# Router products by halves of a tile, value products behind the next tile's scores, six copies moved to VectorE

## The chip, the core and the metric
The kernel runs on one core of a Trainium2 chip. A core has a matrix engine (PE, with its weight loads PEld beside it), VectorE (DVE), ScalarE (ACT), GpSimd (POOL) and a queue engine for transfers (SP). Each engine takes its own instructions in the order in which the program issues them. The metric is the device time in microseconds; all times below are microseconds unless marked otherwise.

## The reference
Three parts follow one another over 2304 tokens (4 sequences of 576) of 512 values:

```python
# 1. attention: 8 heads of 64, each query sees itself and the 63 keys before it
scores = scale * np.matmul(q, k.transpose(0, 1, 3, 2))
scores = np.where((rel >= 0) & (rel < 64), scores, -1e9)
attn = np.exp(scores - np.max(scores, -1, keepdims=True))
attn = attn / (np.sum(attn, -1, keepdims=True) + 1e-09)
x = np.matmul(attn, v)                       # then [2304, 512]
# 2. mixture of 8 experts, two for each token
noisy = x @ w_gate + np.log1p(np.exp(x @ w_noise)) * noise
top2 = ...                                   # the two largest, weights by softmax
out[token] += weight * (np.maximum(x @ w1[e], 0) @ w2[e])
# 3. a feed-forward layer of width 2048 with a piecewise quadratic gate
h = x @ w_in;  g = where(h >= 1, h, where(h <= -1, 0, (h + 1) ** 2 / 4));  return g @ w_out
```

The change touches part 1 and the first line of part 2 only: the router's products `x @ w_gate` and `x @ w_noise` (16 columns together).

## The kernel before
The first 104 us hold the attention with the router and the routing; the experts and the last layer follow and aren't touched.

Attention works on 18 tiles of 128 tokens in 36 steps (`step(u)`, two steps a tile; step u handles heads in the half `u % 2`, and `m = u // 2`). A written order rules: the engines get exactly the order of the calls in `step` (`manual_schedule`). The pieces are:

- `A(i)`, L347 to L366: the scores of a whole tile, for two steps. Four mask products (L355) and 16 products of queries and keys (L364) in 64x64 blocks. A tile's scores fill two of three score banks `Sb`, taken in turn by `u % 3` (L345). Line L364 appears with 32 instructions a tile in the trace, since each f32 product is recorded as two.
- `top(u)`, L371 and L373: the row maxima on VectorE, straight from the score bank; the scaled negative `nb` on GpSimd (from step 4).
- `soft(u)`, L380: four exponentials on ScalarE from the score bank into `p`.
- `C(u)`, L387 and L389: four transposes of `p` on PE into a bank of a pair used in turn (`rot`), and the copy `pt` on ScalarE.
- `Dm(u)`, L401 to L416, for odd u: 16 products of `pt` and the values into `OB` (weights of 128x64, so two column halves), then on VectorE the sums, the reciprocal and the scaled output `x` (L406 to L409), a store of `x`, and a copy of values on GpSimd (L415).
- `Ex(i)`, L422 and L424: four transposes of `x` into a `rot` bank and the copy `xt`, on ScalarE.
- `Gm(i)`, L440 and L443: the router's four products with weights of 128x128 from `xt` and 16 moving columns, into a `rot` bank, and a small copy on VectorE. `logits` calls it, and after the last tile of a group (8, 4 and 6 tiles) starts `route`.
- `route(g)` gives the routing of a group in portions that `advance` takes in each step, mostly on VectorE; it has position products on PE (L558 to L562, in a `rot` bank too) and puts marks (L586, L593) in a queue, which `place` (L634) turns into products.
- `split_w` and `rest_w` (L158, L149) prepare expert weights on ScalarE and VectorE at the ends of some steps (of every four steps, two have a half on ScalarE).

The order in an even step is: `A` of the next tile, `Ex` of the tile two back, `C`, the two `top`, `soft`, `place`, `early`, `advance`, `Dm` of the tile one back with its VectorE part. In an odd step: `C`, `soft`, `logits`, `place`, `early`, `advance`. On ScalarE an even step so has `xt`, `pt`, then the exponentials of `u + 2`. `early` starts the gather for the first expert's rows when the first two groups are placed. After step 36 the last router products stand between transposes for the first expert (L774 to L783).

Of the kernel before, what the change touches and what calls it, by code (L numbers as in the profile page):

```python
# [17 lines left out]
AF = mybir.ActivationFunctionType  # L18
# [8 lines left out]
E, F = 8, 1024  # L27
# [30 lines left out]
def fused_kernel(ctx, tc, qT, kT, v, wg, noise, wcat, out, wd=None):  # L58
    nc = tc.nc
# [41 lines left out]
    def load_qk(j):  # L101
        q_t[j] = qbuf[:, j % 2]
        kt = k_t[j] = qk.tile([P, 4, 320], F32, tag="k", name=f"k{j}")

        for h in (slice(0, P), slice(P, 256)) if j == 0 else (slice(0, 256),):
            t = slice(256 * j + h.start, 256 * j + h.stop)
            nc.sync.dma_start(out=kt[:, :, 64 + h.start:64 + h.stop], in_=kTv[:, :, t])
            nc.sync.dma_start(out=q_t[j][:, :, h], in_=qTv[:, :, t])
        if j == 0:
            nc.vector.memset(kt[:, :, 0:64], 0.0)  # L110


    def keys_before(j):
        nc.gpsimd.tensor_copy(k_t[j][:, :, 0:64], k_t[j - 1][:, :, 256:320])
# [4 lines left out]
    def load_v(i):  # L119
        a = vp.tile([P, H * VW], F32, tag="vE", name=f"vE{i}")  # L120
        nc.sync.dma_start(out=a, in_=v[P * i:P * i + P, :])
        if i == 0:
            vO[0] = vp.tile([P, H * VW], F32, tag="vE", name="vE_")
            nc.vector.memset(vO[0][64:128, :], 0.0)
            nc.sync.dma_start(out=vO[0][0:64, :], in_=v[0:64, :])
        vE[i] = a
# [6 lines left out]
    def load_raw(n, eng=nc.sync):  # L133
        raws[n] = t = raw.tile([P, 1024], F32, tag="raw", name=f"raw{n}")
        if NF <= n < N2:

            if n % NF == 0:
                r = E - 2 if n >= NCE else (n // NF - 1) % (E - 2)
                dyn[n // NF] = nc.values_load(cnt_i[0:1, 1 + r:2 + r], engines=[mybir.EngineType.SP], min_val=0,
                                          max_val=(E - 1) * NF)  # L140
            eng.dma_start(out=t, in_=wcat[bass.ds(dyn[n // NF] + n % NF, 1)].rearrange("o p n -> (o p) n"))
        else:
            eng.dma_start(out=t, in_=wcat[n])
# [114 lines left out]
    wg_sb = ac.tile([P, 4, 32], F32, name="wg_sb")  # L258
# [76 lines left out]
    def rot(u):  # L335
        turn[0] += 1
        return bank[3 + 2 * (turn[0] % 2)] if u <= NU else bank[6]
# [6 lines left out]
    def score(u):  # L344
        return OB[:, 0, :] if u == 3 else Sb[u % 3]  # L345
# [22 lines left out]
    def top(u):  # L368
        mx = wk.tile([P, 4], F32, tag="mx", name=f"mx{u}", bufs=3)
        nb = wk.tile([P, 4], F32, tag="nb", name=f"nb{u}", bufs=3)  # L370
        nc.vector.tensor_reduce(out=mx, in_=score(u).rearrange("p (g n) -> p g n", g=4), axis=AX.X, op=ALU.max)  # L371

        (nc.vector if u < 4 else nc.gpsimd).tensor_scalar(out=nb, in0=mx, scalar1=-0.125, scalar2=None, op0=ALU.mult)  # L373
        mxs[u] = nb

    def soft(u):
        sb, nb = score(u), mxs.pop(u)
        p = wk.tile([P, 4, P], F32, tag="p", name=f"p{u}", bufs=4)
        for g in range(4):
            nc.scalar.activation(p[:, g, :], sb[:, g * P:g * P + P], AF.Exp, bias=nb[:, g:g + 1], scale=0.125)  # L380
        pr[u] = p

    def C(u):
        p = pr.pop(u)
        PTb = rot(u)
        for g in range(4):
            nc.tensor.transpose(PTb[:, g * P:g * P + P], p[:, g, :], idn)  # L387
        t = wk.tile([P, 512], F32, tag="pt", name=f"pt{u}", bufs=PTB)
        nc.scalar.activation(t, PTb, AF.Copy)  # L389
        pts[u] = t  # L390

    def Dm(u):
        i, r = divmod(u, 2)
        if r == 0:
            return
        ts = [pts.pop(2 * i + k) for k in range(2)]
        for h in range(H):
            g, k = divmod(h, 2)
            for c in range(2):
                vv = (vO, vE)[c][i]  # L400
                nc.tensor.matmul(OB[64 * c:64 * c + 64, h // 4, (h % 4) * VW:(h % 4) * VW + VW],  # L401
                                 lhsT=ts[k][:, g * P + 64 * c:g * P + 64 * c + 64], rhs=vv[:, h * VW:h * VW + VW],
                                 start=True, stop=True)
        ov = OB[:, :, 0:4 * VW].rearrange("p b (h d) -> p b h d", d=VW)
        rl = wk.tile([P, 2, 4, 1], F32, tag="rl", name=f"rl{i}")
        nc.vector.tensor_scalar(out=rl, in0=ov[:, :, :, D:VW], scalar1=1e-9, scalar2=None, op0=ALU.add)  # L406
        nc.vector.reciprocal(out=rl, in_=rl)
        x = wk.tile([P, H, D], F32, tag="x", name=f"x{i}", bufs=3)
        nc.vector.tensor_tensor(out=x.rearrange("p (b h) d -> p b h d", b=2), in0=ov[:, :, :, 0:D],  # L409
                                in1=rl.to_broadcast([P, 2, 4, D]), op=ALU.mult)  # L410
        xs[i] = x
        nc.sync.dma_start(out=x_dram[P * i:P * i + P, :], in_=x.rearrange("p h d -> p (h d)"))
        if i + 1 < NT:
            if i + 2 < NT:
                nc.gpsimd.tensor_copy(vE[i][0:64, :], vE[i + 1][0:64, :])  # L415
            vO[i + 1] = vE[i]  # L416

    def Ex(i, u):
        x = xs.pop(i).rearrange("p h d -> p (h d)")
        XTb = rot(u)  # L420
        for k in range(4):
            nc.tensor.transpose(XTb[:, k * P:k * P + P], x[:, k * P:k * P + P], idn)  # L422
        xt = wk.tile([P, 4, P], F32, tag="xt", name=f"xt{i}")
        nc.scalar.activation(xt.rearrange("p k t -> p (k t)"), XTb, AF.Copy)  # L424
        xts[i] = xt

    gstart = [sum(GROUPS[:g]) for g in range(len(GROUPS))]
    n_early = 2 * gstart[EARLY]
# [6 lines left out]
    def Gm(i, u):  # L435
        g, t = tile_group[i]
        xt = xts.pop(i)
        lg = (rot(u) if u <= NU else bank[0])[:, LGO:LGO + 2 * E]
        for k in range(4):
            nc.tensor.matmul(lg, lhsT=xt[:, k, :], rhs=wg_sb[:, k, 0:2 * E], start=(k == 0), stop=(k == 3))  # L440
        if t == 0:
            lgs_g[g] = gp.tile([P, max(GROUPS), 2 * E], F32, tag="lgs", name=f"lgs{g}", bufs=3)
        nc.vector.tensor_copy(lgs_g[g][:, t, :], lg)  # L443
# [179 lines left out]
        state["late"] = True  # L623
        yield 1

    live, rows = [], {}

    def place():
        while pq:
            c, o, ej = pq.popleft()  # L630
            if nids[0] == n_early:
                open_ids()
            nids[0] += 1
            nc.tensor.matmul(IDS2[:, c, :], lhsT=o, rhs=ej, start=False, stop=(nids[0] in (n_early, 2 * NT)))  # L634
# [23 lines left out]
    def open_ids():  # L658
        nc.tensor.matmul(IDS[:, 0:2 * NK], lhsT=wz[:, 0:P], rhs=wz[:, 0:2 * NK], start=True, stop=False)
# [16 lines left out]
    def step(u):  # L676
        for c in range(EW):
            if u == L0 + LS * c:
                load_raw(c)
        if u + 2 < NU:  # L680
            if (u + 2) % 4 == 0 and (u + 2) // 4 + 1 < NT // 2:
                load_qk((u + 2) // 4 + 1)
                keys_before((u + 2) // 4 + 1)
            if (u + 1) % 2 == 0 and (u + 1) // 2 + 1 < NT:
                load_v((u + 1) // 2 + 1)


        m = u // 2
        if u % 2 == 0:
            if u + 2 < NU:  # L690
                A(m + 1)
            if u == NU:
                nc.scalar.activation(vE[NT - 2][0:64, :], vE[NT - 1][0:64, :], AF.Copy)
            if u == NU - 2:
                C(u)
            if 0 <= m - 2 < NT:
                Ex(m - 2, u)
        if u < NU and u != NU - 2:
            C(u)
        if u % 2 == 0 and u + 2 < NU:  # L700
            top(u + 2)
            top(u + 3)
        if u + 2 < NU:
            soft(u + 2)

        if u % 2 == 1 and 0 <= m - 2 < NT:
            logits(m - 2, u)
        place()
        early()
        advance(MARKS[u > NU - 10])  # L710
        if 0 <= u - 1 < NU:
            Dm(u - 1)

        for c in range(EW):
            for h in range(2):
                if u == L0 + LS * c + 3 + h:
                    split_w(c, h)
                if u == L0 + LS * c + 4 + h and c < EW - 2:
                    rest_w(c, slice(512 * h, 512 * h + 512))
            if u == L0 + LS * c + 4 and EW <= c + 2 < NF:  # L720
                load_raw(c + 2)
# [54 lines left out]
    warm(2, Sb[0])  # L776
    xpose("0a", 0, P, Sb[0])
    Ex(NT - 1, NU)
    xpose("0a", 1, P, Sb[1])
    logits(NT - 1, NU)  # L780
# [232 lines left out]
    t0 = 0  # L1013
# [402 lines left out]
    for q, (ui, p) in enumerate(items):  # L1416
# [5 lines left out]
        while ndone < len(items) and ndone <= q + (1 if items[ndone][0] == FIRST2 else 2):  # L1422
            i = items[ndone]
# [84 lines left out]
```

## Time and profile before

| | |
|---|---|
| median of 3 runs | 947.45 (947.38 to 947.93) |
| the profiled execution | 950.02, its span 948.3 |
| PE busy | 935.7, 99% of the span |
| VectorE busy | 665.6, 70% |
| ScalarE busy | 436.5, 46% |
| GpSimd busy | 186.2, 20% |
| TensorE clock granted | 1.0 of full speed in all slices |

Busy times are those of one profiled execution; times in a timeline count from the start of its span. A matmul's end is modelled, so a busy PE can have work overlapping; the weight loads tell better when one group follows another. A bracket at the end of a row is the idle time just before it and what ended it.

### The profile page before, as it was taken

To read this page: it belongs to the slowest core of one execution; us is meant where nothing else is said; L and a number is where in the kernel's file an instruction comes from. 1 tells how busy PE (TensorE), PEld (TensorE's weight loads), DVE (VectorE), ACT (ScalarE), POOL (GpSimd) and SP (SyncE) were. 2 spreads that over 40 slices of the span, in tenths; PEclk is the share of its full clock that TensorE was granted. 3 is DMA by queue.
4 is the path that set the end of the run, shared out by engine and by line. 5 is a ranking of instruction groups with operands and counts; after the bars stand their busy time and mean duration, and the time that the engine had idled before them with its cause. 6 is when DMAs were issued, how large, how long until landed. Compare 5 with 4: busy or idle time off the path is not lost. (4 is left out here: it accounts for less than half of the span.)

```text
span 948.3 us, 17990 instructions
## 1 busy us (share of the span) xinstructions
PE 935.7 (99%) x6779; PEld 832.3 (88%) x6781; DVE 665.6 (70%) x1411; ACT 436.5 (46%) x907; POOL 186.2 (20%) x249
## 2 busy tenths in 40 slices
PE   9999999999999999999999999999999999999998
PEld 6887888988888989898888889988999899899986
DVE  4689765477997968889533366767867776687664
ACT  6898314345565555555433266333433333342221
POOL 3222013133645353354402030000000000000000
PEclk9999999999999999999999999999999999999999
DMA  8874136555888878767725566775576559556521
GB/s 258 300 252 167 56 100 186 188 191 199 290 288 275 261 236 277 257 206 260 252 89 184 204 231 236 252 256 178 177 256 213 164 174 308 175 178 213 182 95 44
DMA packets 91274, 196.95 MB, mean 208 GB/s; under 512 B 7320, under 2 KB 18072, under 8 KB 91184
## 3 DMA queue, kind: packets, MB, share of 16 engines
q1 hardware_dynamic: 83152, 171.68, 54.6%
q0 software_dynamic: 6736, 21.86, 6.4%
q10 hardware_dynamic: 1296, 2.23, 0.6%
q8 instruction: 54, 0.88, 0.4%
q14 instruction: 36, 0.29, 0.1%
HBM read 155.45 MB, written 40.29 MB: 206 GB/s over the span
## 5 line engine op out<-in xcount | busy, mean ns | idle before, releaser
L969 PE MATMUL bank<-wo,hall 128*128 128x512 f32 x864 | 237.6, 394 | 0.0
L969 PE MATMUL bank<-w,hall 128*128 128x512 f32 (+3 forms) x944 | 234.6, 396 | 0.1
L969 PEld LDWEIGHTS bank<-w,hall 128*128 128x128 f32 (+3 forms) x944 | 167.7, 183 | 35.2 <-issue 0.3
L969 PEld LDWEIGHTS bank<-wo,hall 128*128 128x128 f32 x864 | 146.7, 188 | 17.4 <-DVE hall L915 0.2
L904 ACT ACTIVATE hall<-bank 128x288 fp32r<-128x288 f32 (+6 forms) x128 | 54.0, 422 | 218.4 <-PE bank L896 200.6
L896 PE MATMUL bank<-xhie,w 128*128 128x288 f32 (+4 forms) x768 | 122.5, 302 | 0.3 <-DVE hall L907 0.2
L896 PEld LDWEIGHTS bank<-xhie,w 128*128 128x128 f32 x768 | 113.5, 188 | 7.1 <-DVE hall L907 1.4
L907 DVE SCALAR_TENSOR_TENSOR hall<-bank,hall 128x288 fp32r<-128x288 f32 (+7 forms) x168 | 60.0, 391 | 82.5 <-ACT hall L904 75.1
L149 DVE TENSOR_TENSOR w<-raw,w 128x1024 fp32r<-128x1024 f32 (+1 forms) x69 | 81.9, 1188 | 23.8 <-ACT w L158 17.8
L1183 PEld LDWEIGHTS bank<-xb,wi 128*128 128x128 f32 x576 | 80.8, 188 | 8.4 <-DVE cg L1173 0.7
L1207 ACT ACTIVATE hall<-cg 128x512 fp32r<-128x512 f32 x64 | 40.3, 629 | 100.4 <-DVE cg L1205 100.4
L1183 PE MATMUL bank<-xb,wi 128*128 128x256 f32 x576 | 84.3, 282 | 0.3 <-DVE cg L1173 0.3
L1183 PEld LDWEIGHTS bank<-xc,wi 128*128 128x128 f32 x480 | 67.5, 188 | 6.5
L1183 PE MATMUL bank<-xc,wi 128*128 128x256 f32 x480 | 69.9, 280 | 0.0
L158 ACT ACTIVATE w<-raw 128x1024 fp32r<-128x1024 f32 (+1 forms) x71 | 69.4, 977 | 0.0
L896 PE MATMUL bank<-xloe,w 128*128 128x288 f32 (+4 forms) x384 | 69.0, 301 | 0.0
L1201 ACT ACTIVATE mg<-cg 128x512 f32<-128x512 f32 x64 | 40.1, 626 | 45.8 <-DVE cg L1173 44.1
L204 POOL TENSOR_TENSOR td<-rawd 128x512 f32<-128x512 f32 x32 | 33.3, 1040 | 139.6 <-DVE rawd L202 111.8
L896 PEld LDWEIGHTS bank<-xloe,w 128*128 128x128 f32 x384 | 58.0, 188 | 0.0
L1202 DVE SCALAR_TENSOR_TENSOR cg<-mg,cg 128x512 f32<-128x512 f32 x64 | 43.8, 684 | 18.8 <-ACT mg L1201 18.8
L1211 DVE SCALAR_TENSOR_TENSOR hall<-cg,hall 128x512 fp32r<-128x512 f32 x64 | 44.0, 687 | 8.1 <-ACT hall L1207 7.7
L1205 DVE SCALAR_TENSOR_TENSOR cg<-mg,cg 128x512 f32<-128x512 f32 x64 | 44.0, 687 | 1.0
(285 smaller groups left out, 1389.2 us busy)
## 6 DMA issues: line engine op xcount, KB each, us to landing
wi<-w1o SPq DMA_DIRECT2D x56, 1024.0 KB
raw<-wcat SPq DMA_DIRECT2D x64, 512.0 KB
rawd<-wd SPq DMA_DIRECT2D x32, 512.0 KB
w1o<-so SPq DMA_DIRECT2D x64, 256.0 KB
y<-y_dram SPq DMA_DIRECT2D x28, 256.0 KB
vE<-v SPq DMA_DIRECT2D x18, 260.0 KB
x_dram<-x SPq DMA_DIRECT2D x18, 256.0 KB
k<-kT SPq DMA_DIRECT2D x8, 512.0 KB
```

The costliest lines, as they stand in the source:

```text
L149: nc.vector.tensor_tensor(out=w[:, 1, c], in0=t[:, c], in1=w[:, 0, c].bitcast(F32), op=ALU.subtract)
L158: nc.scalar.activation(w[:, 0, c], t[:, c], AF.Copy)
L896: nc.tensor.matmul(ps, lhsT=l[k], rhs=r[:, k, s:s + w], start=(c == 0), stop=(c == len(prods) - 1))
L904: nc.scalar.activation(hh, ps, AF.Relu)
L907: nc.vector.scalar_tensor_tensor(out=t, in0=ps[:, c], scalar=0.0, in1=hh[:, c].bitcast(F32), op0=ALU.max, op1=ALU.subtract)
L969: nc.tensor.matmul(M2[b][0:w], lhsT=h2[:, o:o + w], rhs=r[n], start=(first and a == 0), stop=(last and a == end))
L1183: nc.tensor.matmul(ps, lhsT=w[:, l, k * P:k * P + P], rhs=r[:, m, k, :], start=(c == 0), stop=(c == len(prods) - 1))
L1201: nc.scalar.activation(st["m"], c, AF.Relu, scale=0.5)
L1202: nc.vector.scalar_tensor_tensor(out=c, in0=st["m"], scalar=1.0, in1=c, op0=ALU.min, op1=ALU.subtract)
L1205: nc.vector.scalar_tensor_tensor(out=c, in0=st["m"], scalar=1.0, in1=c, op0=ALU.min, op1=ALU.mult)
L1207: nc.scalar.activation(h2[:, 0:T], c, AF.Copy, scale=-1.0)
L1211: nc.vector.scalar_tensor_tensor(out=h2[:, T:2 * T], in0=c, scalar=-1.0, in1=h2[:, 0:T].bitcast(F32), op0=ALU.mult, op1=ALU.subtract)
```

## The change
The router's products are issued for tokens 0 to 63 and 64 to 127 apart, so eight products with weights of 128x64 in place of four with 128x128. `Dm` loses its VectorE part, the store and the copy of values to a new `norm`, which stays at the end of the step; from step 4 on the products of `Dm` are issued right behind `A` and ahead of `Ex` and `C`. For tiles 0 to 5 the copy `xt` goes to VectorE and is issued behind the two `top` of its step. In odd steps `place` comes before `logits`.

```diff
@@ Dm / norm
                                  start=True, stop=True)
+
+    def norm(u):
+        i, r = divmod(u, 2)
+        if r == 0:
+            return
         ov = OB[:, :, 0:4 * VW].rearrange("p b (h d) -> p b h d", d=VW)
@@ Ex
-        nc.scalar.activation(xt.rearrange("p k t -> p (k t)"), XTb, AF.Copy)
         xts[i] = xt
+        if i < 6:
+            behind_tops.append(lambda: nc.vector.tensor_copy(xt.rearrange("p k t -> p (k t)"), XTb))
+        else:
+            nc.scalar.activation(xt.rearrange("p k t -> p (k t)"), XTb, AF.Copy)
@@ Gm
         for k in range(4):
-            nc.tensor.matmul(lg, lhsT=xt[:, k, :], rhs=wg_sb[:, k, 0:2 * E], start=(k == 0), stop=(k == 3))
+            for t0 in (0, 64):
+                s = slice(t0, t0 + 64)
+                nc.tensor.matmul(lg[s], lhsT=xt[:, k, s], rhs=wg_sb[:, k, 0:2 * E], start=(k == 0), stop=(k == 3))
@@ step
                 nc.scalar.activation(vE[NT - 2][0:64, :], vE[NT - 1][0:64, :], AF.Copy)
+            if u > 2:
+                Dm(u - 1)
             if u == NU - 2:
                 C(u)
@@
             top(u + 2)
             top(u + 3)
+        while behind_tops:
+            behind_tops.popleft()()
         if u + 2 < NU:
             soft(u + 2)
 
+        place()
         if u % 2 == 1 and 0 <= m - 2 < NT:
             logits(m - 2, u)
-        place()
         early()
         advance(MARKS[u > NU - 10])
         if 0 <= u - 1 < NU:
-            Dm(u - 1)
+            if u <= 2:
+                Dm(u - 1)
+            norm(u - 1)
```

## Rows read from the trace of the kernel before
**Rows 1.** The page's first part: busy time, share of the span, instructions.
```profile
PE 935.7 (99%) x6779; PEld 832.3 (88%) x6781; DVE 665.6 (70%) x1411; ACT 436.5 (46%) x907; POOL 186.2 (20%) x249
```
**Rows 2.** Waits of PE from 100 us on: total, times, longest.
```profile
PE bank L761 <- DVE xloe L768: 2.2, 1, 2.2
```
**Rows 3.** Timeline of the weight loads, one tile: start, duration, operation, idle before.
```profile
43.77 0.11 PEld L355 LDWEIGHTS <-id 64*64 64x64 bf16 x4
...
44.99 0.42 PEld L422 LDWEIGHTS bank<-idn,x 128*128 128x128 f32 x4 [0.17 <-ACT p L380]
45.38 0.47 PEld L387 LDWEIGHTS bank<-idn,p 128*128 128x128 f32 x4
46.01 1.01 PEld L401 LDWEIGHTS ob<-vE,pt 128*64 128x64 f32 x32 [0.17 <-issue]
47.09 0.42 PEld L387 LDWEIGHTS bank<-idn,p 128*128 128x128 f32 x4
47.48 0.97 PEld L440 LDWEIGHTS bank<-wg_sb,xt 128*128 128x128 f32 x8
48.48 0.11 PEld L355 LDWEIGHTS <-id 64*64 64x64 bf16 x4
```
**Rows 4.** The same timeline: the first loads of A3 and of A13.
```profile
15.34 0.24 PEld L355 LDWEIGHTS <-id 64*64 64x64 bf16 x4 [0.17 <-issue]
...
62.60 0.11 PEld L355 LDWEIGHTS <-id 64*64 64x64 bf16 x4
```
**Rows 5.** Timeline of all engines in step 2: A waits for a score bank.
```profile
10.62 1.21 ACT L380 ACTIVATE p<-bank,nb 128x128 f32<-128x128 f32 x4
...
11.88 0.40 PE L355 MATMUL bank<-mask,id 64*64 64x512 bf16 x2 [0.85 <-ACT p L380]
...
13.08 0.42 PEld L387 LDWEIGHTS bank<-idn,p 128*128 128x128 f32 x4 [0.17 <-issue]
```
**Rows 6.** Timeline of ACT in the tile of rows 3.
```profile
45.69 0.60 ACT L424 ACTIVATE xt<-bank 128x512 f32<-128x512 f32 x1 [0.91 <-PE bank L422]
46.18 0.59 ACT L389 ACTIVATE pt<-bank 128x512 f32<-128x512 f32 x1
46.66 1.15 ACT L380 ACTIVATE p<-bank,nb 128x128 f32<-128x128 f32 x4
47.65 0.67 ACT L158 ACTIVATE w<-raw 128x512 fp32r<-128x512 f32 x1
48.17 0.63 ACT L389 ACTIVATE pt<-bank 128x512 f32<-128x512 f32 x1
```
**Rows 7.** Timeline of PE in the same tile.
```profile
44.99 0.66 PE L422 MATMUL bank<-idn,x 128*128 128x128 f32 x4
45.48 0.60 PE L387 MATMUL bank<-idn,p 128*128 128x128 f32 x4
```
**Rows 8.** Timeline of DVE in the same tile.
```profile
45.19 1.29 DVE L371 TENSOR_REDUCE mx<-bank 128x4 f32<-128x512 f32 x2 [0.85 <-PE bank L364]
```
**Rows 9.** Groups by line, DVE, 0 to 250 us: busy us, mean ns, idle before.
```profile
L988 DVE COPY ye<-bank 128x512 f32<-128x512 f32 x3 | 2.1, 688 | 1.0 <-PE bank L969 1.0
```
**Rows 10.** Timeline of PE, the position products of the first group.
```profile
67.67 0.19 PE L558 MATMUL bank<-ohs,tri 128*128 128x64 bf16 x1 [0.30 <-ACT pt L389]
```
**Rows 11.** Timeline of DVE in the routing part and the tail.
```profile
69.89 1.28 DVE L371 TENSOR_REDUCE mx<-bank 128x4 f32<-128x512 f32 x2
...
88.13 1.28 DVE L371 TENSOR_REDUCE mx<-bank 128x4 f32<-128x512 f32 x2
...
95.90 0.69 DVE L409 TENSOR_TENSOR x<-ob,rl 128x512 f32<-128x512 f32 x1
```
**Rows 12.** Busy time by stretch: length, PE, PEld, DVE, ACT, POOL, clock, DMA, GB/s.
```profile
70.00:80.00 10.00, 9.73 (x183) 8.36 (x181) 9.76 (x39) 9.97 (x32) 2.20 (x6) 1.00 0.79 286
```
**Rows 13.** Timeline of PE in the tail.
```profile
96.73 0.63 PE L422 MATMUL bank<-idn,x 128*128 128x128 f32 x4 [0.65 <-ACT pt L389]
...
101.46 1.06 PE L440 MATMUL bank<-wg_sb,xt 128*128 128x16 f32 x8 [0.45 <-ACT xt L424]
```

More of the change, by code (lines that the diff above doesn't have):

```diff
@@ L624, in bump @@
         yield 1
-    live, rows = [], {}
+    live, rows, behind_tops = [], {}, deque()
     def place():
```

## The prediction
> **What bounds the kernel now.** I read the page first, then the timeline of the attention stage engine by engine, then the waits in it. The page gives PE 99% busy over the span [rows 1], so the reader should ask of any edit whether PE, which takes its instructions in order, gets to the first feed-forward product earlier or later. After about 104 us PE is filled by the feed-forward and its longest wait there, 2.2 us [rows 2], is for rows gathered by what the routing found, so it too follows from the attention stage: a shift of that stage should move the end by the same amount.
>
> The attention stage runs in pairs of steps, one tile a pair. One pair in the weight loads [rows 3]: masks and scores A at 43.77, turned output Ex 44.99, turned probabilities C 45.38, values Dm 46.01, second C 47.09, router Gm 47.48, next A 48.48. Each group starts as the one before it ends, so this stage is PE's own work: 4.71 a tile. From A3 at 15.34 to A13 at 62.60 [rows 4] it is 47.26 for ten tiles, 4.73 each.
>
> Behind that lies a second loop, which decides here. There are three score banks, and A writes two of them; its third mask product needs the bank whose four exponentials were queued on ACT one pair earlier. That the kernel waits there by name is seen in step 2: exponentials 10.62 + 1.21 = 11.83, mask product at 11.88 with 0.85 idle, released by ACT p [rows 5]. ACT takes its queue in order too: in an even step it does xt (from Ex), then pt (from C), then those exponentials [rows 6]. So the loop is A, Ex, C, pt, exponentials, A. Measured from the release of A's third mask: 1.20 to the next group's load (13.08 less 11.88, [rows 5]); Ex's four products end 0.66 after its load, 45.65 [rows 7]; xt starts 0.04 later (45.69), pt 0.49 after that, the exponentials 0.48 after that, they last 1.15 [rows 6], and A follows 0.05 after: 1.20 + 0.66 + 0.04 + 0.49 + 0.48 + 1.15 + 0.05 = 4.07. The rows agree: exponentials end at 47.81, A starts 48.48, so 0.67 is to spare.
>
> **The change part by part.**
>
> *Values' products moved.* From step 4 on, Dm stands between A and Ex. PE's total isn't changed by it, but the loop is: Dm now lies ahead of C, C ahead of pt, pt ahead of the exponentials for which the next A waits. Queued behind Dm on PE are Ex and both C; who waits for those is ACT, with pt and the exponentials behind. Dm's price is 1.08 (46.01 to 47.09, [rows 3]). New loop, without an xt on ACT: A to Dm 1.20, Dm 1.08, Ex to C 0.39 (44.99 to 45.38), C's load to its last product 0.70 (45.38 to 46.08, [rows 3, 7]), then 0.04, 0.48, 1.15, 0.05 = 5.09. With xt on ACT: 1.20 + 1.08 + 0.66 + 0.04 + 0.49 + 0.48 + 1.15 + 0.05 = 5.15. Both are above 4.73, so the 0.67 is used up and PE stands idle before A.
> The term that no row shows is the turn from A (64x64 blocks) to Dm (128x64). After A the load engine shows 0.17 idle, before Ex as before C [rows 3, 5]; from Gm to A it is only 0.03 (48.45 to 48.48). I take 0.17, the row with the same predecessor; with 0.03 the loops are 4.95 and 5.01.
> Dm's own input is no later wait: the exponentials occupy ACT for 0.99, a weight split for 0.52 (46.66 to 47.65 to 48.17, the pt row [rows 6]), pt 0.63, so the second pt ends about 6.1 after the old release, and Dm needs it at 5.09 + 1.20 = 6.29.
>
> *Router by halves.* 8 loads of 128 columns in 0.97 become 16 of 64 columns. Dm loads 32 of that very shape in 1.01, 0.032 each [rows 3], so 16 take 0.51: 0.46 less. Against it, going from C into 64-column blocks costs 0.63 (45.38 to 46.01) where C to Gm cost 0.39. So PE saves 0.2 net, in a stretch in which, by the loop above, it waits anyway. Worth nothing in the loop; by itself it lies between a gain of 0.22 a tile and a loss of 0.24 (the turn paid and no load shortened).
> The Trainium skill, TensorE: Matmul & The Clock Gate, Part 3 (packing small matmuls), says that a weight load overlaps running products only where the row groups differ. The two halves share all rows, and by that the 16 loads would take as long as the 8 did, a rival below. The trace speaks against it: Dm's 32 loads share all rows too and went at 0.032 each.
>
> *Turned output copied by VectorE, six tiles.* It removes xt from ACT, and in the new order that is worth only the 0.06 between 5.15 and 5.09, since pt waits for C. On DVE it comes behind both maxima (they end 2.71 after A's load: 45.19 + 1.29 less 43.77, [rows 8]), starts when Ex ends (1.20 + 1.08 + 0.66 = 2.94, and 0.13 for the hand-over, my allowance of three times ScalarE's 0.04), and takes 0.69, the nearest copy from PSUM of that shape [rows 9]: done 3.76. The second C takes that bank, so: 3.81, C to Gm 0.63, Gm 0.51, 0.03 = 4.98, under 5.09 by 0.11. That is its cover. The maxima stay ahead of it, and nb on POOL with them.
> Placing ahead of the router costs nothing until step 26, when there are first marks.
>
> *Sum of the light part.* Steps 4 to 14 are six periods of 5.09, steps 16 to 22 four of 5.15: 51.14 against 47.26, +3.9. With the smaller turn 6 x 4.95 + 4 x 5.01 = 49.74, +2.5.
>
> *Routing part, 62.6 to 88.* At the end of step 25 the position product takes the bank of the second C and already waited for its pt (0.30 at 67.67, [rows 10]), 5.07 after A13. In the new order the exponentials start at 3.95 (1.20 + 1.08 + 0.66 + 0.04 + 0.49 + 0.48), so that pt comes at 3.95 + 0.99 + 0.52 = 5.46, ends 6.09, and the product starts 6.14: 1.07 later. VectorE reads it next, so +1.0. From there the maxima come at 69.89 and 88.13 [rows 11], 18.24 for three tiles, 6.08 each, with DVE 9.76 busy of 10 [rows 12]: above 5.15, so VectorE sets this stretch as before and the delay is only handed on. Bounds 0.3 and 1.0.
>
> *Tail.* The last tiles have no A, so Dm ahead is a gain: x for tile 16 came at 96.59 (95.90 + 0.69, [rows 11]) and Ex began at 96.73 after a wait; its row names ACT pt, but x was what came last [rows 13]. With Dm in front, x is ready before, but Dm of the last tile now waits for its pt and ACT's copy of the values first, so most of it is lost: I count 0.3. The router products after 98 stand on PE's path (101.46, [rows 13]) and give 0.4. Together -0.7, bounds 0 and -1.5.
>
> Sum: +3.9 + 1.0 - 0.7 = +4.2. The profiled execution took 950.02 (span 948.3), 2.6 above the median 947.45; the difference is carried to the median: 951.6.
>
> **Rivals.**
> *Faster: the score wait does not bind.* If A did not have to wait for the exponentials behind pt, PE's own sum would rule: 1.22 + 1.08 + 0.39 + 0.39 + 0.63 + 0.54 = 4.25, 0.48 a tile less; ten tiles -4.8, the tail -0.7, time 942. For it: PE at 99% and 0.2 to 0.46 truly removed. Against it: step 2 shows this very wait, and the order on ACT is not altered. It decides from the point at which the exponentials end less than 4.7 after the release. Chance 0.12.
> *No change.* The turn costs 0.03 (+2.5), the delay of the position product is eaten by VectorE's shorter backlog (0), the tail gives its full 1.5: +1.0, 948.5. For it: DVE gets idle time in the light part. Against it: all three must fall one way. Chance 0.10.
> *Slower still: the halves don't overlap.* Then Gm lasts 0.97, and PE's path behind the turned output is 3.81 + 0.63 + 0.97 + 0.03 = 5.44 in six tiles and, with xt on ACT (2.98 + 0.60 + 0.05 = 3.63 in place of 3.81), 5.26 in four: 6 x 0.35 + 4 x 0.11 = 2.5 more, 954.1. Against it stands Dm's pace. Chance 0.08.
>
> **How the numbers follow.** My forecast has 0.70. Its own range is +1.3 (2.5 + 0.3 - 1.5) to +4.9, 948.7 to 952.4. The range takes in no change and the halves without overlap and leaves out the faster case: 947.5 to 954.5. About 0.2% (1.9 us) is what can be told from no change. Slower is the forecast without its low end and the third rival, 0.77; same is the second rival and a little, 0.11; faster 0.12.
>
> **What would show it.** In the light part A to A should read about 5.1, with PE idle 0.3 or more before or inside the masks, released by ACT p; Ex and C should start some 2.3 and 2.7 after A; the router's 16 loads should take about 0.5. DVE should hold six copies of about 0.69 right behind the maxima, with pt no earlier for it. The position product of step 25 should wait longer for pt. I am wrong if A to A is under 4.7 there, or if PE shows no wait for ACT p, or if the stage's loss does not reach the first feed-forward product.

## The result, and the profile after

The changed kernel takes 954.62 (median of 6 executions, 953.81 to 955.12); the kernel before, timed beside it, 947.94 (947.38 to 948.96). The ratio is 1.0072 with a 95% interval of 1.0061 to 1.0083: slower by 6.7 where 4.2 was forecast, and 0.1 above the forecast's range of 947.5 to 954.5. The profiled execution took 953.81.

First the page: busy time, share of the span, instructions [rows 1]. PE is busy for 1.8 less and the span is 3.8 longer, so the change has bought waits.

```profile
span 952.1 us, 18293 instructions
...
PE 933.9 (98%) x6923; PEld 828.3 (87%) x6925; DVE 670.2 (70%) x1417; ACT 433.3 (46%) x901; POOL 185.1 (19%) x249
```

The waits of PE between 15 and 110 us name them (engine, line, bank waited for and releaser: total, times, longest).

```profile
PE bank L387 <- DVE rl L411: 3.0, 6, 0.5
PE bank L568 <- ACT pt L389: 2.1, 2, 1.3
PE bank L387 <- ACT xt L433: 1.3, 5, 0.3
PE bank L644 <- DVE ohe L603: 1.2, 1, 1.2
PE bank L644 <- ACT ohe L606: 1.2, 1, 1.2
PE bank L450 <- ACT xt L433: 1.1, 2, 0.7
```

New line numbers: `Ex` L427, `xt` L431 on VectorE and L433 on ScalarE, sums and scaling L411 to L414, router L450, position products L568, marks L596 to L606, `place` L644. The stage, cut where A's first mask loads, against [rows 4] and the other A's of the same timeline:

| stretch | before | after | difference | forecast |
|---|---|---|---|---|
| start to A3 | 15.34 | 15.06 | -0.28 | 0 |
| A3 to A13, ten light tiles | 47.26 | 51.06 | +3.80 | +3.9 |
| A13 to A14, position products of group 0 | 5.38 | 6.82 | +1.44 | |
| A14 to A17 | 17.02 | 17.65 | +0.63 | |
| A13 to A17, routing part | 22.40 | 24.47 | +2.07 | +1.0 |
| A17 to the first feed-forward load | 18.73 | 19.26 | +0.53 | -0.7 |
| sum, at that load | 103.73 | 109.85 | +6.12 | +4.2 |

The spans differ by only 3.8 because the wait of 2.2 in [rows 2] is absent from the profile after: from that load to the end it takes 842.25 where the profile of before takes 844.58. That profile of before, at 950.02, was 2.1 above the median; so the 6.12 is what to set against the 6.7 between medians, and 0.6 of it is left unassigned.

One tile in the light part, weight loads (start, duration, operation, idle before), as [rows 3]. The first line is the second C of the last tile with `xt` on VectorE; from 48.13 on, `xt` is on ScalarE:

```profile
44.60 0.42 PEld L387 LDWEIGHTS bank<-idn,p 128*128 128x128 f32 x4 [0.71 <-issue]
45.19 0.55 PEld L450 LDWEIGHTS bank<-wg_sb,xt 128*64 128x64 f32 x16 [0.17 <-issue]
45.77 0.18 PEld L355 LDWEIGHTS <-id 64*64 64x64 bf16 x4
...
47.05 1.01 PEld L401 LDWEIGHTS ob<-vE,pt 128*64 128x64 f32 x32 [0.17 <-issue]
48.13 0.42 PEld L427 LDWEIGHTS bank<-idn,x 128*128 128x128 f32 x4
48.52 0.47 PEld L387 LDWEIGHTS bank<-idn,p 128*128 128x128 f32 x4
49.47 0.42 PEld L387 LDWEIGHTS bank<-idn,p 128*128 128x128 f32 x4 [0.49 <-ACT xt L433]
50.06 0.55 PEld L450 LDWEIGHTS bank<-wg_sb,xt 128*64 128x64 f32 x16 [0.17 <-ACT pt L389]
50.63 0.11 PEld L355 LDWEIGHTS <-id 64*64 64x64 bf16 x3
50.99 0.10 PEld L355 LDWEIGHTS <-id 64*64 64x64 bf16 x1 [0.25 <-issue]
...
55.79 0.11 PEld L355 LDWEIGHTS <-id 64*64 64x64 bf16 x3
```

The period is 51.06 / 10 = 5.11 (5.10 each from 25.37 to 45.77; 5.16 from 50.63 to 55.79). The 16 loads of the router take 0.55. In the tile at 50.63 the mask is cut in two: three loads, then 0.25 idle, and the fourth as ScalarE's exponentials end (ACT, as [rows 6]; 49.80 + 1.15 = 50.95):

```profile
48.83 0.60 ACT L433 ACTIVATE xt<-bank 128x512 f32<-128x512 f32 x1 [1.52 <-PE bank L427]
49.32 0.59 ACT L389 ACTIVATE pt<-bank 128x512 f32<-128x512 f32 x1
49.80 1.15 ACT L380 ACTIVATE p<-bank,nb 128x128 f32<-128x128 f32 x4
```

In the tiles with the copy on VectorE the second C waits 0.51 for it (DVE and PE). The row of PE names the next DVE instruction (44.41 to 44.56), but that one reads `OB`; the bank that C takes is the one the copy reads until 44.49:

```profile
43.80 0.69 DVE L431 COPY xt<-bank 128x512 f32<-128x512 f32 x1 [0.40 <-PE bank L427]
```
```profile
44.63 0.63 PE L387 MATMUL bank<-idn,p 128*128 128x128 f32 x4 [0.51 <-DVE rl L411]
```

The score bank still holds A in these tiles, though little: the exponentials end at 45.79 (ACT), and the four mask loads at 45.77 take 0.18 where they take 0.11 in [rows 3].

```profile
44.66 1.13 ACT L380 ACTIVATE p<-bank,nb 128x128 f32<-128x128 f32 x4
```

The routing part and the tail (PE, as [rows 10, 13]): four waits, and behind the last one products that last longer than the same ones elsewhere.

```profile
72.63 0.19 PE L568 MATMUL bank<-ohs,tri 128*128 128x64 bf16 x1 [1.29 <-ACT pt L389]
...
83.59 0.65 PE L644 MATMUL bank<-ohe,ohr 128*128 128x145 f16 x4 [1.17 <-ACT ohe L606]
...
90.39 0.18 PE L568 MATMUL bank<-ohs,tri 128*128 128x32 bf16 x1 [0.77 <-ACT pt L389]
...
96.06 0.65 PE L644 MATMUL bank<-ohe,ohr 128*128 128x145 f16 x4 [1.17 <-DVE ohe L603]
96.64 0.65 PE L450 MATMUL bank<-wg_sb,xt 128*64 128x16 f32 x16
97.23 1.56 PE L401 MATMUL ob<-vE,pt 128*64 128x65 f32 x32
98.73 1.12 PE L387 MATMUL bank<-idn,p 128*128 128x128 f32 x4
99.64 1.06 PE L427 MATMUL bank<-idn,x 128*128 128x128 f32 x4
```

By stretch (columns as [rows 12]; the number behind POOL's is the granted clock): from 70 to 80 VectorE has 8.27 of 10 where it had 9.76, from 90 to 97 PE is 5.36 busy of 7, and from 98 to 101 it has half the clock, 1.2 GHz; by the rows on either side, from 97.8 to 101.2.

```profile
70.00:80.00 10.00, 8.37 (x187) 7.10 (x189) 8.27 (x35) 8.92 (x28) 1.43 (x5) 1.00 0.64 225
...
80.00:90.00 10.00, 8.37 (x154) 6.98 (x150) 9.51 (x48) 8.68 (x26) 2.03 (x6) 1.00 0.45 152
...
90.00:97.00 7.00, 5.36 (x105) 4.43 (x106) 6.79 (x27) 5.52 (x18) 1.09 (x3) 1.00 0.25 78
...
97.00:98.00 1.00, 1.00 (x33) 0.99 (x33) 0.61 (x5) 0.83 (x4) 0.00 (x0) 0.89 0.05 18
98.00:101.00 3.00, 3.00 (x26) 2.72 (x24) 1.81 (x7) 0.86 (x2) 1.94 (x2) 0.50 0.39 102
101.00:102.00 1.00, 1.00 (x20) 0.83 (x18) 0.00 (x0) 0.72 (x2) 0.70 (x2) 0.90 0.60 162
```

### The profile page after: what moved, and what is told of

The parts are those of the page before. It is cut to its first block, busy times and chain, and to the rows that moved or that the text cites. A ratio compares the mean times of both kernels' runs of the same rounds, so it can differ in the third digit from the quotient of the medians.

```text
span 952.1 us, 18293 instructions
## 1 busy us (share of the span) xinstructions
PE 933.9 (98%) x6923; PEld 828.3 (87%) x6925; DVE 670.2 (70%) x1417; ACT 433.3 (46%) x901; POOL 185.1 (19%) x249
```

## The experiments

The theory: the values' products, put ahead of C, lengthen the loop through the score bank, and the routing part pays on top. The rivals: the loss is the halves' or the copies', or the routing's and the clock's alone. Every ratio is to runs of the kernel before on the same chip (medians 951.0, 950.8, 947.8 and 951.2 in the four groups below), so ratios, not times, compare across groups, and those only roughly: the changed kernel itself has 1.0072 in the result and 1.0095 in the third group. Stretches of one trace can be set against another's, but a median holds more than the attention stage. The wait of [rows 2] stands in some traces (2.0 to 2.2) and not in others, sometimes with a stretch at half clock behind it, and from the first feed-forward load to the end the traces differ by up to 6.6 (842.25 to 848.84).

### First group: the parts alone

**Halves alone**, put into the kernel before:

```diff
-            nc.tensor.matmul(lg, lhsT=xt[:, k, :], rhs=wg_sb[:, k, 0:2 * E], start=(k == 0), stop=(k == 3))
+            for t0 in (0, 64):
+                s = slice(t0, t0 + 64)
+                nc.tensor.matmul(lg[s], lhsT=xt[:, k, s], rhs=wg_sb[:, k, 0:2 * E], start=(k == 0), stop=(k == 3))
```


> The kernel before with the router's products by halves and nothing else. Theory (the loss comes from the value products standing ahead of the even step's transposes, so that pt, the exponentials and the next A come later): here the order is the old one, the loop over the score bank stays 4.07 us against about 4.5 of PE work, so PE sets the tile: router 0.55 in place of 1.00, the turn into it 0.24 dearer, 0.2 less a tile where PE sets it, 0.9 more from the last router products; 944 to 946 against 947.9, A to A near 4.5. Rival (the halves cost: turns between block shapes, or loads that don't overlap): router loads near 0.97, A to A at 4.7 to 5.0, 948 to 951.


Measured 951.61, ratio 1.0005 (0.9992 to 1.0018): no gain. Where nothing waits, A follows A after 4.48 (4.71 before), so the 0.2 a tile is real; but A6 to A7 takes 6.08, since the queries have not landed (PE):

```profile
31.22 1.10 PE L364 MATMUL bank<-k,qbuf 64*64 64x128 f32 x32 [1.37 <-DMA qbuf<-qT]
```

PE waits 3.3 for `qbuf` in all, in three places (1.37, 0.20 and, in the routing part, 1.70), and none in the profile of before. Ten tiles faster by 0.2 meet a transfer that was just hidden: A3 to A13 takes 46.98, only 0.28 less. The profiled execution was the dearest of its twelve (956.55), so the amount is not typical.

**Values' products alone**, put into the kernel before (with `norm` split off, the router whole, `xt` on ScalarE):

```diff
+            if u > 2:
+                Dm(u - 1)
             if u == NU - 2:
                 C(u)
...
-            Dm(u - 1)
+            if u <= 2:
+                Dm(u - 1)
+            norm(u - 1)
```


> The kernel before with the value products alone moved behind A (with the VectorE part left at the end of the step); router undivided, xt on ScalarE, marks placed where they were. Theory: the loop over the score bank is 5.15 in every tile, PE waits for ACT p inside the masks, the position product waits over 1 us for pt; 953 to 957 against 947.9. Rival (the loss comes from the halves or from the copies on VectorE): PE has the same work in another order, so A to A stays near 4.7 and the time within 1.5 us of 947.9.


Measured 958.76, ratio 1.0076 (1.0060 to 1.0093): this part alone costs the whole loss. From A4 at 20.03 to A13 at 66.41 each tile takes 5.15 or 5.16. PEld shows two of them:

```profile
30.34 0.14 PEld L355 LDWEIGHTS <-id 64*64 64x64 bf16 x4
...
34.01 0.42 PEld L387 LDWEIGHTS bank<-idn,p 128*128 128x128 f32 x4 [0.49 <-ACT xt L429]
34.49 0.97 PEld L445 LDWEIGHTS bank<-wg_sb,xt 128*128 128x128 f32 x8
35.49 0.14 PEld L355 LDWEIGHTS <-id 64*64 64x64 bf16 x4
```

With the router whole PE has little idle time, and the period is the same as with halves: what the halves save is given back as waiting. By itself this run does not tell the two loops apart: the four mask loads take 0.14 for 0.11, so the score bank holds A by 0.03 only, and the path through `xt`, the second C and the whole router is almost as long. The tiles from 50.63 on in the changed kernel tell them apart, where the router is short and A is held all the same. The routing part of this trace also has a stretch at half clock, from 72.5 on (A14 to A15 6.62, 5.07 before).

**The rest alone**: the changed kernel with `Dm` and `norm` back at the end of the step.

```diff
-            if u > 2:
-                Dm(u - 1)
...
-            if u <= 2:
-                Dm(u - 1)
-            norm(u - 1)
+            Dm(u - 1)
```


> The changed kernel with the value products and their VectorE part back at the end of the step; halves, six copies on VectorE and marks ahead of the router kept. Theory: the loss is gone and the gain of the halves is left, A to A near 4.5 in the light part; 943 to 947 against 947.9 and 954.6. Rival (copies on VectorE hold the bank of the second C, or marks ahead of the router hold PE up, whatever the order): A to A at 4.9 to 5.1 in the first six tiles, 950 to 954.


Measured 951.73, ratio 1.0013 (0.9998 to 1.0028). The loss is gone, so neither the halves nor the copies cause it. The gain that I expected did not come either: A to A takes 4.48 to 4.72 with two long ones between (28.51 to 33.64, 47.28 to 53.35), in which PE halts within A's products and the profile names no releaser (0.97 before a product at 49.07). What holds it there stays open.

**The wait taken away another way**: `pt` of even steps behind the exponentials, all `xt` on ScalarE, so that A need not wait for exponentials behind `pt`.

```diff
-        nc.scalar.activation(t, PTb, AF.Copy)
...
+        if u % 2 == 0 and 2 < u < NU - 2:
+            behind_soft.append(lambda: nc.scalar.activation(t, PTb, AF.Copy))
+        else:
+            nc.scalar.activation(t, PTb, AF.Copy)
```


> The changed kernel with pt of each even step behind that step's exponentials on ScalarE, and all xt copies on ScalarE as before the change; value products still ahead. Theory: A no longer waits for the exponentials (they start when nb is there, about 2.4 after the release, or when xt is done, 3.5); what is left is the second C that waits for xt's bank: 2.98 + 0.60 + 0.05 + 0.63 + 0.57 = 4.8 a tile in the light part in place of 5.1, so 3 us less there: 950.5 to 952.5. Rival (the loop over the score bank is not what binds, PE's wait comes from elsewhere): A to A stays at 5.1 and the time at 954 to 955.


Measured 966.07, ratio 1.0151 (1.0130 to 1.0172): a miss. A no longer waits, but `pt` also frees the bank that the router takes, and that wait is longer (PE, then ACT):

```profile
49.82 0.65 PE L450 MATMUL bank<-wg_sb,xt 128*64 128x16 f32 x16 [0.86 <-ACT pt L391]
50.40 0.41 PE L355 MATMUL bank<-mask,id 64*64 64x512 bf16 x4
```
```profile
48.15 1.14 ACT L380 ACTIVATE p<-bank,nb 128x128 f32<-128x128 f32 x4
49.15 0.62 ACT L391 ACTIVATE pt<-bank 128x512 f32<-128x512 f32 x1
49.62 0.63 ACT L393 ACTIVATE pt<-bank 128x512 f32<-128x512 f32 x1
```

A to A is 5.74 here (44.66 to 50.40): the order on ScalarE has two consumers, and swapping them hands the wait to the other.

### Second group: the routing part and the clock

**The kernel before once more**, unchanged, for a second trace of it.


> The kernel before once more, for its trace beside the others. If the halves alone gained nothing because the tiles then wait for their queries and keys, this trace should show A to A at 4.7 with no or little wait of PE for qbuf, and the clock 1.0 through the attention stage, as the first trace does; if instead this chip is short of transfers for every order, the kernel before waits for qbuf too, by about 1 us or more.


One execution, 954.65, well above the median of the others (950.84). It has a wait of 1.44 for `qbuf` (PE; 1.37 in the halves' trace), and longer products behind it (1.12 for the 0.66 of [rows 7]), at half clock from 82.3 on: so the kernel before stands close to that edge too, and the low clock is not the change's alone. Six of the seven other executions of the kernel before in this group have a mean clock of 0.998 or more, so this one is no typical one.

```profile
81.30 1.13 PE L364 MATMUL bank<-k,qbuf 64*64 64x128 f32 x32 [1.44 <-DMA qbuf<-qT]
82.37 1.12 PE L422 MATMUL bank<-idn,x 128*128 128x128 f32 x4
```

**Placing behind the router again**, in the changed kernel:

```diff
-        place()
         if u % 2 == 1 and 0 <= m - 2 < NT:
             logits(m - 2, u)
+        place()
```


> The changed kernel with the marks placed behind the router again in odd steps. Theory (PE waits 1.17 us for marks in steps 29 and 33 with the router queued behind): the router goes first, 0.55 less in step 33, and in step 29 nothing in the end since VectorE sets the next maxima: 0.3 to 0.8 less than the changed kernel, ratio to before 1.006 to 1.007. Rival (the order of placing decides the loss in the routing part): 2 us less, ratio 1.005.


Measured 955.85, ratio 1.0052 (1.0035 to 1.0068), below what the theory expected and near the rival's 1.005. The two waits of 1.17 become 0.59 and 0.60, A15 to A16 takes 6.18 in place of 6.62. So half of each wait was the router held back behind it, and half is the marks', which come late in either order. In the step where nothing was expected (step 29, A15 to A16) 0.44 is won. The clock still fell (0.91 and 0.92 in 90 to 110), here behind waits of 0.60 and 0.68 (PE):

```profile
97.24 1.27 PE L401 MATMUL ob<-vE,pt 128*64 128x65 f32 x32 [0.68 <-DVE first L470]
```

**Position products in a spare part of `OB`**, so that they don't wait for the bank of `pt`, in the changed kernel:

```diff
-        pos = (rot(0) if g < EARLY else bank[0])[:, POS:POS + T * E]
+        pos = (OB[:, 1, :] if g < EARLY else bank[0])[:, POS:POS + T * E]
```


> The changed kernel with the position products of the first two groups in a spare part of the output banks, so that they don't wait for pt to leave the second transposes' bank. Theory: step 25's wait (1.29) goes, the next A comes when its exponentials are done, 1.3 earlier, and VectorE hands this on to the end of the stage; step 31's wait (0.77) goes too but there VectorE's marks set the pace: 1.0 to 2.0 less than the changed kernel, ratio to before 1.0050 to 1.0062. Rival (VectorE's own work sets the routing part from its start): no change, 1.0072.


Measured 956.87, ratio 1.0064 (1.0048 to 1.0081). A13 to A14 takes 5.88 in place of 6.82: the wait of 1.29 at step 25 was the bank's. At step 31 the product then waits 1.17 for `x`, which reads `OB`, in place of 0.77, and A13 to A17 falls by 0.56 only (24.47 to 23.91): the 0.94 is not handed on whole, as the theory had it.

**Five products of zeros ahead of the wait at 94.9**, in the changed kernel, to keep PE busy there:

```diff
+        if u == NU - 3:
+            warm(5, Sb[0])
         place()
```


> The changed kernel with five products of zeros (128 by 512) on PE into a free score bank ahead of the wait for marks in step 33. Theory (the stretch at the lower clock, 97.9 to 101.4 us, follows the idle time at 94.9 to 96.1 and costs about 1.4): the idle time is filled, the granted clock stays 1.00 through the stage, 1 to 1.5 less than the changed kernel, ratio to before 1.0056 to 1.0062. Rival (the lower clock comes from the whole routing part's idle time, or costs nothing since VectorE and ScalarE set the tail): the low stretch stays or moves, within 0.4 of the changed kernel.


Measured 958.19, ratio 1.0074 (1.0047 to 1.0100): no gain to be seen, and the spread is wide. The four executions follow their mean granted clock: 955.72 at 1.000, 957.40 at 0.998, 958.98 at 0.996 (the profiled one), 960.87 at 0.994. In the profiled one the low clock is gone from 97 to 101 and stands behind the wait of step 25 instead (PE), with a second stretch from 161.5 on, behind the wait for gathered rows:

```profile
72.16 0.19 PE L568 MATMUL bank<-ohs,tri 128*128 128x64 bf16 x1 [1.29 <-ACT pt L389]
...
72.70 1.84 PE L364 MATMUL bank<-k,qbuf 64*64 64x128 f32 x32
74.47 1.94 PE L401 MATMUL ob<-vE,pt 128*64 128x65 f32 x32
```

The stretch from A14 to A15 takes 6.51 where it takes 5.19 after: a fall costs 1.3 here. The tail, with the clock whole, takes 18.80 in place of 19.26, with a wait of 1.06 for gathered rows in it. Up to step 33 this kernel issues what the changed kernel issues, whose trace keeps 1.00 behind the same wait of 1.29: so which of the waits the clock falls behind differs from one execution to another, and I can't say by what rule. With four executions and one trace the theory of the zeros is neither shown nor refuted.

### Third group: does the sum close?

**The changed kernel once more**, on the chip of this group.


> The changed kernel once more, on the same chip as the two variants of it that follow. Theory: A3 to A13 takes 51.1 us again, the routing part waits 1.3 for pt in step 25 and 1.2 for marks in step 29, and one stretch at the lower clock follows one of the waits of over 1 us; ratio to before 1.006 to 1.008. Rival (the loss in the routing part and the lower clock were accidents of one execution): the stage ends 1.5 to 2 us earlier than in the first trace, ratio 1.005.


Measured 956.43, ratio 1.0095 (1.0080 to 1.0110), above the 1.006 to 1.008 expected. Same waits (1.29, 1.17, 0.78, 1.18), first feed-forward load at 110.43, A13 to it 43.74 (43.73 in the first trace); granted clock 0.93 and 0.90 in 90 to 110. None of the eleven executions of the changed kernel on record has a mean clock above 0.998.

**Both mendings of the routing part together** (placing behind the router, position products in `OB`; the two diffs above).


> The changed kernel with both: marks behind the router, position products in the spare part of the output banks. Theory (routing part costs 2.1 by the pt wait and the marks ahead of the router): A13 to the first feed-forward product falls from 43.7 to about 42.5, what is left against before is the light part's 3.8; 1.0 to 1.6 less than the changed kernel on the same chip. Rival (VectorE's own work sets this part, waits on PE cost nothing): within 0.5 of the changed kernel.


Measured 952.49, ratio 1.0055 (1.0040 to 1.0069): 3.9 less than the changed kernel beside it, where 1.0 to 1.6 was expected. The light part is as before this mending (A3 to A13 51.08), A13 to A17 takes 23.46, and the clock holds (windows, clock 1.00), so A17 to the first feed-forward load takes 18.11. By parts: +3.8, +1.06 (23.46 less 22.40), -0.62 (18.11 less 18.73): +4.2, with 4.7 measured between medians. Against the trace of the changed kernel beside it the first feed-forward load comes 2.3 earlier (108.14 for 110.43); the rest of the 3.9 lies behind it or in other executions. Four of the five executions have a mean clock of 1.000, the fifth 0.998.

```profile
96.00:98.00 2.00, 1.49 (x37) 1.29 (x35) 1.84 (x9) 1.28 (x5) 0.22 (x1) 1.00 0.33 119
98.00:100.00 2.00, 1.69 (x21) 1.35 (x21) 0.92 (x3) 1.17 (x3) 1.70 (x2) 1.00 0.29 41
```

**Halves, with expert weights every five steps** in place of four, in the kernel before, to free transfer time for `qbuf`:

```diff
-EW, L0, LS, F0 = 7, 1, 4, 1
+EW, L0, LS, F0 = 7, 1, 5, 1
```


> The kernel before with the halves and with the expert weights' loads and splits five steps apart in place of four. Theory (the halves' 0.23 a tile is lost because the transfers of queries, keys, values, outputs and weights can't come faster than one tile in about 4.65): with a fifth of the weight traffic less, A to A stays at 4.48 without a wait for qbuf, 2 us less in the light part, of which VectorE takes up to 1.4 back since two more weight rests fall into the routing part; 0 to 2 less than before. Rival (the waits for qbuf come from the order of the queue, not from the rate): a wait of over 1 us for qbuf stays in the light part, time as with the halves alone.


Measured 947.46, ratio 0.9997 (0.9987 to 1.0007). The waits for `qbuf` fall to 0.5 in all and A3 to A13 takes 45.99, 1.27 less than before. But the weights' last rests now fall into the routing part, and A13 to A17 takes 24.15, 1.75 more. The tail takes 17.29, 1.44 less, so the first feed-forward load comes at 102.51, 1.2 ahead of the profile of before; of that the medians show 0.36, within the noise.

**Halves, with the router right behind the values' products** in even steps, in the kernel before:

```diff
-        if u % 2 == 1 and 0 <= m - 2 < NT:
-            logits(m - 2, u)
...
             Dm(u - 1)
+            if u % 2 == 0 and 0 <= m - 2 < NT - 2:
+                logits(m - 2, u)
```


> The kernel before with the halves, and the router of a tile issued right behind the value products in even steps, so that two groups with 64-column weights stand together. Theory (transfers bound the light part once PE needs under 4.6): PE's own sum falls to about 4.3 but A to A averages 4.5 or more, with waits for qbuf; within 1 us of the halves alone. Rival (PE sets the light part): A to A 4.3 without waits, 3 to 4 us less than before.


Measured 947.13, ratio 0.9994 (0.9984 to 1.0004). Staying among 64-column blocks makes a tile 4.33 where nothing waits; the gain goes into waits of 2.3 for `qbuf` and 2.9 of the position products for a VectorE copy: A3 to A13 takes 46.31.

### Fourth group: what would release the halves' gain

**As the spaced kernel, with two of the late rests on GpSimd:**

```diff
...
-                    rest_w(c, slice(512 * h, 512 * h + 512))
+                    rest_w(c, slice(512 * h, 512 * h + 512), nc.gpsimd if c > 2 else nc.vector)
```


> The kernel before with the halves, loads and splits of the expert weights five steps apart, and the last two of the five early weight rests on GpSimd in place of VectorE. Theory (with the halves the light part gains 1.3 and VectorE's work sets the routing part, where two more rests cost 1.75 from A13 to A17): four rests of 0.69 leave VectorE there, A13 to A17 goes back to 21.5 to 22.5, the light gain reaches the end: 1.3 to 2.5 less than before, ratio 0.9973 to 0.9987. Rival (something else than VectorE sets the routing part, or GpSimd's rests delay the scaled maxima behind them): A13 to A17 stays at 23.5 to 24.5, ratio 0.999 to 1.001.


Measured 951.20, ratio 0.9994 (0.9985 to 1.0004). A13 to A17 takes 23.66: a miss, only 0.5 of the 1.75 came back. What else holds the routing part there stays open; ScalarE, 9.72 busy of 10 from 70 to 80, is a candidate that I did not test. The first feed-forward load comes at 101.84, 1.9 ahead of the profile of before, but the rest takes 847.64, 3.1 more than there: at the end of the wait for gathered rows (2.17, until 152.1) begins a stretch at half clock, from 152.0 to 155.4. So part of the gain was there and was lost behind the stage. No kernel tried is clearly faster than the one before.

## Why the prediction was off, step by step

- **The score-bank loop: right.** Putting `Dm` ahead of C makes the light part 5.11 a tile (forecast 5.09 and 5.15), 51.06 in all (51.14), and the products alone give 5.15 or 5.16 in each tile. The rival in which that wait does not bind is out, and so is the rival in which nothing can be told. The sign that I gave for it, idle of 0.3 or more on PE released by ACT p, is not to be found in that form: no such wait is in the list between 15 and 110. In the four tiles from 50.63 on the load of the fourth mask comes 0.36 behind the first, as the exponentials end; in the five from 25.37 to 45.77 A is held by 0.07, and the long idle stands ahead of the second C.
- **The turn to 64-column blocks: right.** 0.17 ahead of `Dm` after A, the larger of my two bounds. The Trainium skill, TensorEngine Tiling (Array Packing), Key Properties, says that a change of tiling mode drains TensorE; the trace agrees at this turn, with 0.17 idle of the weight loads, while from the router (128x64) to A (64x64) only 0.03 lie between the loads.
- **The halves overlap: right.** 16 loads took 0.55 (forecast 0.51) where 8 took 0.97. The Trainium skill, TensorE: Matmul & The Clock Gate, Part 3, lets a load overlap running products only where row groups differ; these differ in their columns alone, so by it, as an estimate, they should have taken 0.97, and the measurement decides against it. The rival in which they don't overlap is out.
- **The copy on VectorE: right, with less cover.** I gave its path 4.98, 0.11 under the loop. It started 3.13 after A's first load (43.80 less 40.67) where I had 3.07, and the second C began 3.93 after it (44.60) where I had 3.81; in both, 0.07 is what the score bank holds A. Without these 0.07 the path is 5.03 (3.86, and 0.59 and 0.58 to the next A). So it has 0.07 of cover left, and the score-bank loop sets the period in these tiles too. The maxima were done 0.40 before the copy started, so it was Ex and the hand-over that it waited for.
- **Routing part, first step that failed:** "pt comes at 3.95 + 0.99 + 0.52 = 5.46, ends 6.09, and the product starts 6.14: 1.07 later". It started 6.51 after A13's load (72.63 less 66.12), 1.44 later. The 0.37 too few lie at the loop's origin: I counted from the release of A's third mask as if the first mask loaded at that time, but three masks load ahead of the held one (50.63 against 50.99 above, 0.36). The same slip did no harm in the light part, where only periods count. The spare-bank run took 0.94 off that stretch.
- **Routing part, second step that failed:** "VectorE sets this stretch as before and the delay is only handed on." From 70 to 80 VectorE was 8.27 busy of 10: it was kept waiting there, and from 80 on, at 9.51, it did not make that up. (The reading was weak already: in the same row [rows 12] ScalarE was busier than VectorE, 9.97 of 10.) A14 to A17 grew by 0.63 more, and what grew is A15 to A16, 6.62 for 5.78, where PE waits for marks. On ScalarE the marks of step 29 stand behind exponentials which `Dm` has pushed back (82.09 + 1.15 = 83.24, so they start 3.96 after A15; before the change 3.06, first row below), VectorE's last one is there at 83.40, and the mark product starts at 83.59; with `place` ahead, the router stood queued behind that wait. I had written that placing ahead costs nothing until there are marks, and priced nothing from there on. The runs with placing behind the router, alone and with the spare bank, show it: 0.4 of the 0.84 on A15 to A16.

```profile
76.11 1.14 ACT L380 ACTIVATE p<-bank,nb 128x128 f32<-128x128 f32 x4
```
```profile
82.09 1.15 ACT L380 ACTIVATE p<-bank,nb 128x128 f32<-128x128 f32 x4
```

- **Tail: the step that failed is "Together -0.7".** Measured +0.53. What I left out is TensorE's clock. PE was 5.36 busy of 7 from 90 to 97, with a wait of 1.17 in it, and then had 1.2 GHz from 97.8 to 101.2: `Dm` 1.56 for 1.15, C 1.12 and Ex 1.06 for 0.66. Each of the two mendings alone leaves that stretch in and the tail at 19.30 and 19.40; with both, the trace has no such stretch and the tail takes 18.11, 0.62 under before. So by these traces the stretch is worth about 1.2, and with both mendings the gain that I forecast is there; in the run with products of zeros a fall cost 1.3, and the tail, at the full clock, took 18.80 with the wait of 1.06 in it. A forecast that adds idle time to PE has to allow for it. Why the clock held with both mendings stays open: the length of the waits does not tell, for with the marks alone put back the clock fell behind waits of 0.60 and 0.68, and with both mendings it held behind one of 1.29 (at 89.84).

With both mendings the parts (+3.8, +1.06, -0.62) come close to the forecast's (+3.9, +1.0, -0.7), but for the routing part that is luck: the forecast's +1.0 was the wait of the position product for `pt`, which that kernel no longer has. Of the change itself the forecast missed 1.1 in the routing part and 1.2 in the tail. That a shift of the stage moves the end by the same amount held between the medians (6.7 for 6.12) and not between the two profiles (3.8), since the wait behind the stage came in one of them alone.

## What to carry to other kernels

Before moving work ahead on an in-order engine, close the loop through each buffer that the next round waits for, and price everything on the other engines that then comes later, small marks and copies included: the longest loop sets the period, and saved work off that loop is only waited away. Take the loop's origin at the instruction that waits, not at the first of its group. And where a change adds idle time to TensorE, look for a stretch at half clock behind it, in more than one execution: here it came and went between executions.

## What the runs showed of the hardware that was not expected

- Weight loads of 128x64 in alternating column halves overlap: 0.034 a load (16 in 0.55) where those of 128x128 take 0.121 (8 in 0.97). A single load of 128x64 is recorded with 0.138, so several run at once.
- Waits of PE were followed by a stretch at half clock in some places (1.17 at 96.06, 1.29 in the run with zeros, 1.44 in the second trace of before, 0.60 and 0.68 with the marks put back) and in others not (1.29 at 72.63 and 1.17 at 83.59, with 1.00 granted from 70 to 90). The wait of 2.0 to 2.2 for gathered rows behind the stage was followed by one in seven traces and not in three. In the attention stage such a stretch cost 1.2 to 1.3.
- The light part has little room in its transfers: in stretches of 10 us from 25 to 55 the kernel before moves 287 to 291 GB/s without a wait, the halves alone 256 to 301 with waits of 1.37 and 0.20 for queries, for 0.2 less work a tile.
- One weight rest of 128x512 is recorded with 1.27 on GpSimd and 0.69 on VectorE (the run with two rests on GpSimd; spans on GpSimd are rough).
